# A table of places instead of a scheduler, from unit 8 on, and Pool's subtractions in halves

## The chip, the cores and the metric

The kernel runs on one core of a Trainium2 chip. The metric is the device time of one execution in microseconds; lower is better. A profile adds the busy time of each engine: TensorE (PE, with its weight loads as PEld), VectorE (DVE), ScalarE (ACT), GpSimd (POOL), and SP, which here only issues transfers.

## What is computed

A delta rule attention over 4 batches, 8 heads, 768 tokens of 48 numbers, and behind it a feed-forward layer (384 to 2048 to 384) with a rational function between its two products:

```python
for t in range(S):
    kt, vt, bt = (k_n[:, :, t], v[:, :, t], beta[:, :, t, None])
    y[:, :, t] = np.einsum('bhd,bhde->bhe', q[:, :, t], state)
    v_old = np.einsum('bhde,bhd->bhe', state, kt)
    state = state + bt[:, :, :, None] * np.einsum('bhd,bhe->bhde', kt, vt - v_old)
...
h = x @ w_in
h2 = h * h
h3 = h2 * h
P = a[0] + a[1] * h + a[2] * h2 + a[3] * h3
Q = 1.0 + np.abs(b[0]) * np.abs(h) + np.abs(b[1]) * h2
g = P / (Q + 1e-06)
return (g @ w_out).astype(np.float32)
```

`k_n` is `k` divided by its norm, and `x` is the attention's output with the heads side by side, 3072 rows of 384.

## The kernel before

**Tiling.** The 768 tokens are cut into 12 chunks of 64. One chunk of all four batches makes 256 rows for the feed-forward layer, whose 2048 hidden columns are cut into 8 units of 256. So there are 96 units, numbered through; unit 27 is unit 3 of chunk 3. Every number is kept as a pair of float16 (a rounded part and what is left), and a product of two such pairs is three matmul passes (`PASSES`).

**A unit.** `hidden` (L806) makes the first product in 18 matmuls into `ph`. `numerator` gives ScalarE two instructions (L826, L827) and a third (L829), and VectorE three (L828, L830, L831); `quotient` gives ScalarE Ln and Exp (L839, L840), VectorE L842 (which writes the first half of `mg`), L843 and L844, and Pool L845 (the second half of `mg`). `accumulate` (L860) is the second product, 12 matmuls in three groups of four into `po`. L843 uses the `ph` of the next unit as scratch, so the first product of a unit two later waits until L844 has read it (two `ph` buffers). `in_order` keeps these VectorE instructions in the order in which they are written.

**Attention.** Each chunk runs ahead of the units that use it, in stages of some instructions on each engine. Keys: load `kw`, normalize (`keys_normalized`, L481 to L492), transpose (`ptk`, L448, with a correction by `minus16`, L464), move to block-diagonal form by a transfer (`kbd`), multiply (`pg`, L396), write to memory and read back in another layout (`gd`, `gb`). The inverse of 16x16 blocks on VectorE (L543 to L576) goes out and back through `img` and `wc`. Queries likewise (`ptq`, `pm`, `mm`). Then the recurrence: split the state (`sh`), residual (`pk`, `v`, `rr`), three solve steps and a last one (`pu`, `z`, L238), the new state (`pd`, L703), the outputs (`py`, `y`), and the tokens (L734 to L746), which find a scale for `x` in seven hand-overs between ScalarE, TensorE and VectorE. All attention products go through `mm3` (48 matmuls each, L396). `split16` (L228 to L241) makes the float16 pair: ScalarE rounds, and VectorE, or Pool where `eng=nc.gpsimd` is given, subtracts (L236).

**What sets the order.** The kernel is traced in loops: for each unit `n` the numerator of `n`, the quotient of `n - 1`, one step of the attention stages (`back`, `middle`, `front`, `ahead`, each for another chunk), the second product of `n - 2`, the first product of `n + 1`. The tracing framework then schedules all of it: it runs a list scheduler with its own estimate of each instruction's duration over the whole program and picks, engine by engine, what is ready, with `tc.high_priority` for the recurrence. So the order that the chip gets is that scheduler's, and it differs from chunk to chunk. Each engine works through its queue in order; transfers are issued by SP, in order too.

Of the kernel before, what the change touches and what calls it, by code (L numbers as in the profile page):

```python
# [36 lines left out]
def kernel(  # L37
# [191 lines left out]
    def split16(dst, src, scale=None, eng=None):  # L229
# [5 lines left out]
        if scale is None:  # L235
            (eng or nc.vector).tensor_sub(dst[1], src, dst[0])  # L236
        else:
            nc.vector.scalar_tensor_tensor(  # L238
                out=dst[1], in0=src, scalar=scale, in1=dst[0], op0=ALU.mult, op1=ALU.subtract
            )  # L240

# [800 lines left out]
```

## Time and profile before

| | us |
|---|---|
| median of 3 runs (lowest to highest) | 833.21 (831.11 to 839.61) |
| the profiled execution | 836.04 |
| its span, first to last instruction | 834.3 |
| busy: DVE, ACT, PE, POOL | 720.0, 652.7, 649.7, 296.4 |
| first ScalarE instruction of unit 0, 8, 80 | 148.5, 222.9, 749.6 |

Busy time is time with at least one instruction on the engine. Instructions of one engine overlap at their ends, so that a queue without gaps has its starts closer together than one instruction takes. The clock that TensorE was granted averaged 0.958 of full speed. The chain that ended last is followed back from the last instruction, at each step to what released it.

### The profile page before, as it was taken

The page shows a single profiled execution, that of the slowest core. Times are in us where ns is not written, and L with a number is a line of the kernel's source. Part 1 is how long each engine was busy: PE and PEld are TensorE (multiplying, and loading weights), DVE is VectorE, ACT ScalarE, POOL GpSimd, SP SyncE. Part 2 cuts the span into 40 slices and gives each one's busy share as a digit, 9 for nine tenths or more (in the row PEclk, how much of TensorE's full clock was granted, in tenths as well). Part 3 has the DMA queues.
Part 4 walks back from the last instruction along what each step waited for, and adds up shares of the span by engine and source line. Part 5 has one row for each costly group of instructions (what it writes and reads, how often), then busy time and mean ns, then how long its engine had stood idle before and what let it go on. Part 6 is the DMA issues. An engine that isn't in the chain of part 4 may idle for free.

```text
span 834.3 us, 23340 instructions
## 1 busy us (share of the span) xinstructions
PE 649.7 (78%) x9520; PEld 514.5 (62%) x9520; DVE 720.0 (86%) x1290; ACT 652.7 (78%) x1301; POOL 296.4 (36%) x263
## 2 busy tenths in 40 slices
PE   1323465677889788888988998889989988998995
PEld 1213454565677676666776776667858867686662
DVE  5787768988979888779998889999989898998996
ACT  4755678889877986878987978879879776887973
POOL 7451425225233443323513514522433231322232
PEclk9999975999989999999999999999999999999998
DMA  8977867566467646685467275275455353200000
GB/s 224 214 141 177 212 147 141 97 96 116 77 108 131 93 97 103 97 137 97 73 136 116 49 135 103 58 137 90 100 98 95 78 86 66 54 2 21 1 20 20
DMA packets 358411, 84.35 MB, mean 101 GB/s; under 512 B 349856, under 2 KB 352928, under 8 KB 358304
## 3 DMA queue, kind: packets, MB, share of 16 engines
q1 hardware_dynamic: 356128, 81.69, 52.0%
q8 instruction: 75, 1.23, 0.6%
q10 hardware_dynamic: 2176, 1.17, 0.5%
q14 instruction: 32, 0.26, 0.1%
HBM read 34.70 MB, written 13.65 MB: 58 GB/s over the span
## 4 chain that ended last, share of the span: by engine, by line
DVE 28%; PE 24%; DMA 18%; ACT 15%; SPq 7%; issue 5%; POOL 1%; POOLq 0%; ACTq 0%; DVEq 0%
PE ph L806 8%; PE po L860 6%; DVE ph L843 3%; PE pu L396 3%; DVE mx L831 3%; DVE mg L842 2%; DMA qw<-in_q_dram 2%; SPq L604 2%; SPq L122 2%; DVE mx L828 2%; DMA gd<-g 2%; DVE mx L844 2%; DVE mx L830 2%; DMA wc<-img 2%; DMA img<-wh 2%
## 5 line engine op out<-in xcount | busy, mean ns | idle before, releaser
L806 PE MATMUL ph<-xT,w_in 128*128 128x256 f16 x1728 | 214.4, 278 | 28.3 <-DVE mx L844 18.3
L860 PE MATMUL po<-w_out,mg 128*128 128x384 f16 x1152 | 222.7, 334 | 16.3 <-DVE mg L842 10.0
L845 POOL TENSOR_TENSOR mg<-mx 128x512 f16<-128x512 f32 x96 | 125.1, 1303 | 306.0 <-DVE mx L844 236.1
L806 PEld LDWEIGHTS <-w_in 128*128 128x128 f16 x1728 | 168.7, 100 | 62.2 <-issue 19.9
L860 PEld LDWEIGHTS <-mg 128*128 128x128 f16 x1152 | 108.2, 99 | 83.0 <-DVE mg L842 15.6
L828 DVE SCALAR_TENSOR_TENSOR mx<-mx,msc,ph 128x512 f32<-128x512 f32 x96 | 71.2, 742 | 23.9 <-ACT mx L827 18.8
L843 DVE SCALAR_TENSOR_TENSOR ph<-mx,msc,mg 128x512 f32<-128x512 f32 x96 | 84.3, 878 | 0.8
L396 PEld LDWEIGHTS <-kbd 128*128 128x128 f16 x1680 | 59.3, 102 | 38.4 <-issue 29.6
L829 ACT ACTIVATE mx<-mx 128x512 f32<-128x512 f32 x96 | 60.7, 632 | 27.8 <-DVE mx L828 27.5
L826 ACT ACTIVATE mx<-ph,msc 128x512 f32<-128x512 f32 x96 | 65.3, 680 | 13.7 <-PE ph L806 6.7
L842 DVE SCALAR_TENSOR_TENSOR mg<-mx,msc 128x512 f16<-128x512 f32 x96 | 74.9, 781 | 0.4 <-ACT mx L840 0.4
L827 ACT ACTIVATE mx<-ph,coef,msc 128x512 f32<-128x512 f32 x96 | 74.3, 774 | 0.0
L844 DVE SCALAR_TENSOR_TENSOR mx<-mx,msc,ph 128x512 f32<-128x512 f32 x96 | 71.3, 743 | 1.3
L831 DVE SCALAR_TENSOR_TENSOR mx<-mx,msc,ph 128x512 f32<-128x512 f32 x96 | 71.2, 741 | 1.0
L839 ACT ACTIVATE mx<-mx,msc 128x512 f32<-128x512 f32 x96 | 69.4, 723 | 1.4
L830 DVE TENSOR_TENSOR mx<-ph,mx 128x512 f32<-128x512 f32 x96 | 65.6, 684 | 0.0
L840 ACT ACTIVATE mx<-mx 128x512 f32<-128x512 f32 x96 | 60.5, 630 | 1.0
L396 PEld LDWEIGHTS <-ebd 128*128 128x128 f16 x1728 | 52.5, 99 | 10.6 <-issue 8.1
L396 PE MATMUL pu<-z,ebd 128*128 128x48 f16 x1728 | 53.5, 188 | 6.3 <-DMA ebd<-et 2.8
L396 PEld LDWEIGHTS <-wbd 128*128 128x128 f16 x1152 | 36.3, 100 | 19.5 <-issue 15.9
L236 POOL TENSOR_TENSOR mm<-m,mm 128x1024 f16<-128x1024 f32 x12 | 29.7, 2474 | 52.2 <-ACT mm L232 22.8
L396 PE MATMUL pg<-tk,kbd 128*128 128x64 f16 x576 | 24.2, 204 | 21.9 <-ACT nrm L486 7.8
(197 smaller groups left out, 1234.0 us busy)
## 6 DMA issues: line engine op xcount, KB each, us to landing
wsi<-in_moe_w_in_dram SPq DMA_DIRECT2D x8, 768.0 KB, 7.9
gd<-g SPq DMA_DIRECT2D x24, 256.0 KB, 3.5
wso<-in_moe_w_out_dram SPq DMA_DIRECT2D x8, 768.0 KB, 5.8
mbd<-mm SPq DMA_DIRECT2D x24, 256.0 KB, 4.9
wc<-img SPq DMA_DIRECT2D x24, 256.0 KB, 4.8
wbd<-wc SPq DMA_DIRECT2D x24, 256.0 KB, 4.8
knbd<-kn SPq DMA_DIRECT2D x44, 128.0 KB, 2.9
kw<-in_k_dram SPq DMA_DIRECT2D x48, 96.0 KB, 3.3
```

The costliest lines, as they stand in the source:

```text
L396: nc.tensor.matmul(dst[p][:, h], head(bd, lp, p * H + h), head(rt, rp, p * H + h), start=start and n == 0 and h == 0, stop=stop and n == l ...
L806: nc.tensor.matmul(ph[:, i], w_in[:, f2, wp, cc, i * P : (i + 1) * P], x[:, xp, cc], start=k == 0, stop=k == 3 * NCC - 1,)
L827: nc.scalar.activation(u, ph, AF.Identity, scale=A3, bias=a2)
L828: in_order(nc.vector.scalar_tensor_tensor(out=w, in0=z, scalar=B0, in1=ph, op0=ALU.add, op1=ALU.mult))
L830: in_order(nc.vector.tensor_mul(u, ph, u))
L831: in_order(nc.vector.scalar_tensor_tensor(out=u, in0=u, scalar=A1, in1=ph, op0=ALU.add, op1=ALU.mult))
L839: nc.scalar.activation(r, w, AF.Ln, bias=Q0)
L842: in_order(nc.vector.scalar_tensor_tensor(out=g[:, 0], in0=u, scalar=A0, in1=r, op0=ALU.add, op1=ALU.mult))
L843: in_order(nc.vector.scalar_tensor_tensor(out=t, in0=w, scalar=Q0, in1=g[:, 0], op0=ALU.add, op1=ALU.mult))
L844: in_order(nc.vector.scalar_tensor_tensor(out=u, in0=u, scalar=A0, in1=t, op0=ALU.add, op1=ALU.subtract))
L845: nc.gpsimd.tensor_mul(g[:, 1], u, r)
L860: nc.tensor.matmul(po[p], g[:, gp, i, p * P : (p + 1) * P], w_out[:, f2, wp, i], start=f2 == lo and i == 0 and k == 0, stop=f2 == hi - 1 a ...
```

## The change

Every stage becomes a generator that yields between its pieces, and a table gives each piece a place in units, relative to the chunk (`PLAN`) or to the unit (`UNIT`). All pieces of all chunks are sorted by place and traced in that order. Up to place 8 the framework's scheduler still orders them; from there on a `manual_schedule` for TensorE, VectorE, ScalarE and Pool keeps the traced order as it is. SP's transfers are still placed by the scheduler. The priorities are gone (`FIRST` is empty). The arithmetic stays the same; where Pool subtracts, it does so in two halves. Two small moves: in `numerator`, VectorE's multiplications that follow are now a stage of their own (`cubic`) and L830's counterpart comes ahead of L828's; and in the chunk's scales `v` is squared ahead of `q`.

```diff
         if scale is None:
-            (eng or nc.vector).tensor_sub(dst[1], src, dst[0])
+            n = src.shape[1] // 2
+            for sl in [slice(0, 2 * n)] if eng is None else [slice(0, n), slice(n, 2 * n)]:
+                (eng or nc.vector).tensor_sub(dst[1][:, sl], src[:, sl], dst[0][:, sl])
...
+    def halved(dst, src, scale=None, eng=None):
+
+        if scale is None:
+            nc.scalar.copy(dst[0], src)
+            yield
+            n = src.shape[1] // 2
+            for sl in [slice(0, 2 * n)] if eng is None else [slice(0, n), slice(n, 2 * n)]:
+                if eng is not None and sl.start:
+                    yield
+                (eng or nc.vector).tensor_sub(dst[1][:, sl], src[:, sl], dst[0][:, sl])
...
+    PLAN = {
+        "load_k": (-32.4564,),
...
+        "kbd": (-25.2603,),
...
+        "gram": (-24.5307, -24.311, -23.3642),
...
+        "tokens": (-4.308, -4.1793, -4.0913, -4.0867, -3.9637, -3.8515, -3.7149, -3.7003, -3.4793, -3.3379),
...
+    UNIT = {
+        "hidden": (-0.3166,),
+        "numerator": (0.0001, 0.3411, 0.9473),
+        "cubic": (0.3156, 0.5071),
+        "quotient": (1.343, 1.5094, 1.6629, 1.9614, 2.1316, 2.297),
+        "accumulate": (2.1777, 2.825, 3.0308, 3.1137),
+    }
...
+    def do(event):
+        t, nm, n, last, made = event
+        if not made:
+            made.append(STAGES[nm](n) or iter(()))
+        with tc.high_priority(FIRST[nm]) if nm in FIRST else nullcontext():
+            if last:
+                run(made[0])
+            else:
+                next(made[0], None)
+
+    events = [e for c in range(NCH) for e in of_chunk(c)] + [e for n in range(N) for e in of_unit(n)]
+    events.sort(key=lambda e: e[0])
...
+    upto = 8.0
+    for e in events:
+        if 0 <= e[0] < upto:
+            if e[1:3] == ("hidden", GRP):
+                tables(GRP, NU)
+                scalars(0, GRP, NU)
+            do(e)
+    if upto < N:
+        with tc.manual_schedule(engines={mybir.EngineType.DVE, mybir.EngineType.Activation, mybir.EngineType.PE, mybir.EngineType.Pool}):
+            for e in events:
+                if e[0] >= upto:
+                    do(e)
```

What this moves, at three places. In the names `z_5_1` is step 1 of chunk 5's solve, `mx29` and `mg29` belong to unit 29, and a last number counts buffers.

VectorE from unit 29's second instruction up to unit 30's first, before:

```order
L830 TENSOR_TENSOR mx29_6111<-ph_29_6092,mx29_6111 128x512
L238 SCALAR_TENSOR_TENSOR z_5_0_6300<-pu_5_6198,zmask_91,z_5_0_6300 128x768
L257 TENSOR_SCALAR sf_4_6060<-lgx4_6067 128x1
L756 RECIPROCAL kp_4_0_6125<-lgx4_6067 128x1
L831 SCALAR_TENSOR_TENSOR mx29_6111<-mx29_6111,msc_3_5028,ph_29_6092 128x512
L842 SCALAR_TENSOR_TENSOR mg28_6120<-mx28_6044,msc_3_5028 128x512
L739 RECIPROCAL sf_4_6060<-sf_4_6060 128x1
L482 TENSOR_REDUCE nrm_8_6770<-sq_8_6771 128x16
L843 SCALAR_TENSOR_TENSOR ph_29_6092<-mx28_6044,msc_3_5028,mg28_6120 128x512
L238 SCALAR_TENSOR_TENSOR xT_4_6058<-px_4_6062,sf_4_6060,xT_4_6058 128x768
L844 SCALAR_TENSOR_TENSOR mx28_6044<-mx28_6044,msc_3_5028,ph_29_6092 128x512
```

The same stretch now, from behind the third instruction of unit 29 to the first of unit 30:

```order
L858 RECIPROCAL kp_4_0_6062<-kp_4_0_6062 128x2
L257 SCALAR_TENSOR_TENSOR z_5_1_6248<-pu_5_6087,zmask_91,z_5_1_6248 128x768
L949 SCALAR_TENSOR_TENSOR mg28_6258<-mx28_6023,msc_3_5445 128x512
L616 TENSOR_TENSOR pr_6_5794<-ab_6_5795,wt0_121 128x64 x2
L621 TENSOR_REDUCE wt0_121<-pr_6_5794 128x2x4x4
L951 SCALAR_TENSOR_TENSOR ph_29_6068<-mx28_6023,msc_3_5445,mg28_6258 128x512
L610 TENSOR_TENSOR pr_6_5794<-gb_6_5738,wt0_121 128x512
L613 TENSOR_REDUCE ab_6_5795<-pr_6_5794 128x64
L953 SCALAR_TENSOR_TENSOR mx28_6023<-mx28_6023,msc_3_5445,ph_29_6068 128x512
L616 TENSOR_TENSOR pr_6_5794<-ab_6_5795,wt0_121 128x512
L621 TENSOR_REDUCE wt0_121<-pr_6_5794 128x8x8
L257 SCALAR_TENSOR_TENSOR z_5_2_6347<-pu_5_6087,zmask_91,z_5_2_6347 128x768
```

Two solve steps and most of chunk 6's inverse (`pr_6`, `ab_6`, `wt0`) now share one unit, and the same rows come back every 8 units.

ScalarE from unit 27's first instruction on, before:

```order
L826 ACTIVATE mx27_5932<-ph_27_5913,msc_3_5028 128x512
L827 ACTIVATE mx27_5932<-ph_27_5913,coef_105,msc_3_5028 128x512
L232 CAST mm_6_5648<-m32_6_5646 128x8x2x64
L461 CAST tk_7_5668<-ptk_7_5669 128x4x2x64 x2
L716 ACTIVATE y_4_5886<-py_4_5789,sc_4_3157 128x768
L829 ACTIVATE mx27_5932<-mx27_5932 128x512
L246 ACTIVATE xT_4_6058,xs_4_6059<-y_4_5886 128x768
L839 ACTIVATE mx27_5932<-mx27_5932,msc_3_5028 128x512
L826 ACTIVATE mx28_6044<-ph_28_6025,msc_3_5028 128x512
```

and now:

```order
L922 ACTIVATE mx27_5847<-ph_27_5755,msc_3_5445 128x512
L923 ACTIVATE mx27_5847<-ph_27_5755,coef_105,msc_3_5445 128x512
L488 CAST tq_6_5783<-ptq_6_5784 128x4x2x64 x2
L793 ACTIVATE y_4_5857<-py_4_5554,sc_4_3076 128x768
L497 CAST tq_6_5783<-ptq_6_5784 128x4x2x64 x2
L943 ACTIVATE mx26_5667<-mx26_5667,msc_3_5445 128x512
L945 ACTIVATE mx26_5667<-mx26_5667 128x512
L247 CAST kn1_117<-kw_78 128x4x2x48
L247 CAST rr_5_5979<-v_5_3899 128x768
L269 ACTIVATE xT_4_6000,xs_4_6001<-y_4_5857 128x768
L928 ACTIVATE mx27_5847<-mx27_5847 128x512
L922 ACTIVATE mx28_6023<-ph_28_5981,msc_3_5445 128x512
```

The queries' transposes, the outputs `y`, the residual's rounding and the squares of the tokens stand in one unit; the unit's own third instruction (L928) comes last, ahead of the next unit, and Ln and Exp of the unit before stand in the middle.

Pool around the same units, before:

```order
L845 TENSOR_TENSOR mg24_5465<-mx24_5320 128x512
L236 TENSOR_TENSOR mm_6_5648<-m32_6_5646,mm_6_5648 128x8x2x64
L845 TENSOR_TENSOR mg25_5731<-mx25_5456 128x512
L845 TENSOR_TENSOR mg26_5941<-mx26_5722 128x512
L236 TENSOR_TENSOR rr_5_5999<-v_5_3772,rr_5_5999 128x768
L845 TENSOR_TENSOR mg27_6053<-mx27_5932 128x512
```

and now:

```order
L253 TENSOR_TENSOR rr_5_5979<-v_5_3899,rr_5_5979 128x384
L955 TENSOR_TENSOR mg26_5977<-mx26_5667 128x512
L253 TENSOR_TENSOR rr_5_5979<-v_5_3899,rr_5_5979 128x384
L253 TENSOR_TENSOR kn1_117<-kw_78,kn1_117 128x2x2x48
L253 TENSOR_TENSOR mm_6_6152<-m32_6_6004,mm_6_6152 128x4x2x64
L955 TENSOR_TENSOR mg27_6066<-mx27_5847 128x512
L253 TENSOR_TENSOR mm_6_6152<-m32_6_6004,mm_6_6152 128x4x2x64
L955 TENSOR_TENSOR mg28_6258<-mx28_6023 128x512
```

The subtractions `mm` and `rr` are two instructions each, with a unit's own Pool instruction between the halves.

More of the change, by code (lines that the diff above doesn't have):

```diff
@@ L240, in split16, with run @@
             )
+    def halved(dst, src, scale=None, eng=None):
[8 more added lines that the diff above has]
+        else:
+            nc.scalar.activation(dst[0], src, AF.Copy, scale=scale)
+            yield
+            nc.vector.scalar_tensor_tensor(
+                out=dst[1], in0=src, scalar=scale, in1=dst[0], op0=ALU.mult, op1=ALU.subtract
+            )
+    def run(stage):
+        for _ in stage:
+            pass
     def parts(t):
@@ L582, in inverse @@
             )
+        yield
         im = img[c % NIMG]
@@ new lines @@
+    STAGES = {
+        "load_k": loading("k"),
+        "keys": keys_normalized,
+        "rows": keys_by_row,
+        "load_v": loading("v"),
+        "load_q": loading("q"),
+        "kbd": keys_transposed,
+        "gram": key_products,
+        "gl": key_product_halves,
+        "inverse": inverse,
+        "scales": scales,
+        "queries": queries_transposed,
+        "masked": query_products,
+        "gbd": gram_to_diagonal,
+        "blocks": off_blocks,
+        "wbd": inverse_to_diagonal,
+        "state": state_split,
+        "residual": residual,
+        "qbd": queries_to_diagonal,
+        "mbd": masked_to_diagonal,
+        "knbd": rows_to_diagonal,
+        "solve": solve,
+        "next": state_next,
+        "outputs": outputs,
+        "tokens": tokens,
+        "scalars": scalar_steps,
+        "numerator": numerator,
+        "cubic": cubic,
+        "quotient": quotient,
+        "accumulate": accumulate,
+        "hidden": hidden,
+    }
@@ new lines, in of_chunk, with of_unit @@
+    def of_chunk(c):
+        for nm, times in PLAN.items():
+            if c == 0 and nm in ("state", "qbd", "scalars") or c == NCH - 1 and nm in ("rows", "knbd", "next"):
+                continue
+            if c == 0 and nm == "residual":
+                times = times[2:]
+            made = []
+            for i, t in enumerate(times):
+                yield NU * c + t, nm, c, i == len(times) - 1, made
+    def of_unit(n):
+        for nm, times in UNIT.items():
+            made = []
+            for i, t in enumerate(times):
+                yield n + t, nm, n, i == len(times) - 1, made
@@ new lines @@
+    early = [e for e in events if e[0] < 0]
+    for nm in ("load_k", "load_q", "load_v"):
+        for e in early:
+            if e[1:3] == (nm, 0):
+                do(e)
+    early = [e for e in early if e[2] or e[1][:4] != "load"]
+    for e in early:
+        if e[2] == 0 and e[1] != "hidden":
+            do(e)
+    weights(0, GRP)
+    tables(0, GRP)
+    scalars(0, 0, GRP)
+    weights(GRP, NU)
+    for e in early:
+        if e[2] or e[1] == "hidden":
+            do(e)
+    upto = 8.0
```

350 lines of the change are left out of this document (180 added, 170 removed).

## The prediction

> **What bounds the kernel now.** I read the page's busy times first, then its chain, then the busy times in stretches cut at the first ScalarE instruction (L826) of units 8, 16, 24 and so on, one row for each chunk of eight units. The profiled execution took 836.04 us with a span of 834.3; the median of the runs is 833.21, so a sum made on the span is carried over as a difference.
>
> ```profile
> span 834.3 us, 23340 instructions
> PE 649.7 (78%) x9520; PEld 514.5 (62%) x9520; DVE 720.0 (86%) x1290; ACT 652.7 (78%) x1301; POOL 296.4 (36%) x263
> ...
> DVE 28%; PE 24%; DMA 18%; ACT 15%; SPq 7%; issue 5%; POOL 1%; POOLq 0%; ACTq 0%; DVEq 0%
> ```
>
> No engine bounds the whole: VectorE is busiest with 86%, but the chain that ends last passes through four engines, and a quarter of it (DMA 18%, SPq 7%) is transfers and the queue that issues them.
>
> ```profile
> core 0: us, PE busy (x) PEld busy (x) DVE busy (x) ACT busy (x) POOL busy (x), PEclk, DMA share, GB/s
> 222.90:288.50 65.60, 54.27 (x844) 43.17 (x841) 58.88 (x101) 52.58 (x104) 25.31 (x25) 0.95 0.69 115
> 288.50:356.30 67.80, 57.85 (x981) 47.30 (x982) 54.53 (x99) 54.57 (x106) 26.42 (x23) 1.00 0.56 96
> 356.30:416.50 60.20, 53.07 (x806) 41.50 (x803) 54.98 (x101) 50.16 (x102) 24.93 (x21) 0.97 0.61 101
> 416.50:475.40 58.90, 52.02 (x831) 42.09 (x829) 52.97 (x90) 49.48 (x97) 21.89 (x19) 0.97 0.58 101
> 475.40:537.10 61.70, 53.47 (x795) 42.74 (x790) 56.50 (x103) 49.22 (x101) 23.17 (x20) 0.94 0.51 97
> 537.10:593.30 56.20, 49.33 (x794) 40.17 (x790) 51.55 (x86) 47.32 (x95) 18.73 (x17) 1.00 0.59 106
> 593.30:647.50 54.20, 49.25 (x754) 39.34 (x752) 49.88 (x89) 46.23 (x91) 16.67 (x12) 0.97 0.53 100
> 647.50:706.10 58.60, 52.80 (x918) 42.87 (x915) 53.63 (x93) 44.61 (x84) 15.29 (x11) 0.97 0.43 78
> 706.10:749.60 43.50, 41.85 (x560) 32.88 (x559) 40.75 (x65) 36.52 (x69) 13.13 (x10) 1.00 0.14 32
> 749.60:787.30 37.70, 34.22 (x329) 24.46 (x327) 33.60 (x58) 32.19 (x64) 8.93 (x7) 1.00 0.05 12
> 787.30:834.30 47.00, 36.48 (x246) 23.16 (x244) 37.98 (x53) 28.03 (x44) 13.09 (x10) 0.94 0.07 17
> ```
>
> The reader is to see three things. Chunks 1 to 8 take 54.2 to 67.8 us each, 483.2 in all (60.4 each). TensorE, VectorE and ScalarE are all busy 45 to 58 us of that: three engines with nearly equal work. So the time of a chunk is decided by how well the order interleaves the three, which is what the change rewrites. From chunk 9 on little attention is left (chunk 10: 37.7 us with VectorE at 33.6), and there is little to win.
>
> **What the new order does to each unit.** Both kernels run the same arithmetic, so I price an order by what it puts between the starts of two neighbouring units on each engine. The price of an instruction is its spacing to the next one when that follows at once, since neighbours overlap:
>
> ```profile
> 575.57 0.74 DVE L842 SCALAR_TENSOR_TENSOR mg<-mx,msc 128x512 f16<-128x512 f32 x1
> 576.23 1.01 DVE L238 SCALAR_TENSOR_TENSOR xT<-px,sf,xT 128x768 f16<-128x768 f32 x1
> 577.16 0.75 DVE L843 SCALAR_TENSOR_TENSOR ph<-mx,msc,mg 128x512 f32<-128x512 f32 x1
> ...
> 571.09 0.67 ACT L826 ACTIVATE mx<-ph,msc 128x512 f32<-128x512 f32 x1
> 571.66 0.77 ACT L827 ACTIVATE mx<-ph,coef,msc 128x512 f32<-128x512 f32 x1
> 572.33 0.29 ACT L759 ACTIVATE kp<-top,kp 128x1 f32<-128x1 f32 x1
> ...
> 577.05 1.21 PE pu L396 x48
> 578.26 1.30 PE po L860 x8
> 579.56 1.01 PE pg L396 x34
> 580.57 1.97 PE ph L806 x18
> ```
>
> VectorE: 0.66 us for 128x512, 0.93 for 128x768. ScalarE: 0.57 and 0.67 for the first two of a unit. TensorE: 1.97 for a unit's first product (18 matmuls), 0.65 for four of the second, 1.21 for an attention product of 48. A unit alone is 6 x 0.65 = 3.9 on VectorE, 2.9 on ScalarE, 3.9 on TensorE.
>
> In the new order a chunk has the same eight places each time. By places 0 to 7, TensorE/VectorE/ScalarE in us: 5.1/4.9/3.2, 5.1/4.8/4.8, 5.1/6.0/4.9, 9.0/6.4/8.0, 4.8/7.0/5.1, 7.6/9.1/7.7, 5.1/4.9/7.1, 6.6/4.9/6.1. Two of them worked out: place 3 on TensorE, from unit 27's first product to unit 28's, holds 18 first-product matmuls (1.97), three groups of four second-product ones (1.95), eight transposes (0.87 at 0.109 each, as in the 18), three attention products of 48 (1.21 twice, and 1.4 for the wider one, as 34 of pg take 1.01) and four corrections with minus16 (0.44, at 0.109), 9.0 in all. Place 5 on VectorE is the second order piece of the change: with the three instructions of unit 29 ahead of it, six unit instructions (3.9), two 128x768 for the solve (1.86), and the eight instructions of the inverse (3.3), 9.1 in all. Taking the busiest engine of each place: 5.1 + 5.1 + 6.0 + 9.0 + 7.0 + 9.1 + 7.1 + 6.6 = 55.0 us a chunk.
>
> The old order, counted the same way, is ragged. Chunk 4, unit by unit, busiest engine: 6.9, 9.6, 5.6, 8.3, 5.6, 5.9, 6.0, 10.5, which is 58.4, against 58.9 measured (the row 416.50:475.40). Over chunks 1 to 10 it counts 545 (62.4, 62.7, 61.7, 58.4, 56.6, 56.4, 54.0, 53.6, 41.7, 37.8), and those chunks took 564.4, so waits add a factor of 1.035. The new order counts 515.4 there (55.5, then 54.9 five times, 54.4, 51.2, 44.5, 35.1); times 1.035 is 533.4, a gain of **31 us**. Units are not walls: queues let one engine's long unit overlap another's. If only pairs of units count, the old order is 519.9 and the new 504.5, the factor 1.086, the gain 16.7 us. If only whole chunks count, 473.3 and 463.0, factor 1.193, gain 12 us. The new gain lies between 12 and 31; I take **26**, nearer the single unit, whose factor is nearest to one and holds chunk by chunk.
>
> **The start.** Up to unit 8 the scheduler still orders the work, and the weight loads stand in the same order on the DMA queue. But the new order puts more in front of unit 8's first ScalarE instruction: 157.1 against 153.0 us on ScalarE, 154.1 against 151.9 on VectorE, 82.1 against 73.2 on TensorE, which has the room:
>
> ```profile
> 0.00:148.50 148.50, 57.29 (x823) 48.56 (x823) 108.60 (x219) 95.81 (x207) 65.27 (x73) 0.91 0.78 177
> 148.50:222.90 74.40, 57.80 (x887) 46.28 (x888) 66.19 (x141) 66.02 (x146) 23.60 (x21) 0.93 0.58 98
> ```
>
> TensorE is busy 115 of these 222.9 us, VectorE 175. The added work is what chunk 1 no longer holds. I take **+4 us** (0 to +9). The end (chunk 11: 36.4 against 37.1) I cost at nothing: the same units in the same order, VectorE and TensorE cover each other.
>
> **Pool's halves.** VectorE is held while Pool works, if it reads two operands from SBUF:
>
> ```profile
> 557.96 2.82 DVE L843 SCALAR_TENSOR_TENSOR ph<-mx,msc,mg 128x512 f32<-128x512 f32 x1
> 557.87 2.36 POOL L236 TENSOR_TENSOR mm<-m,mm 128x1024 f16<-128x1024 f32 x1 [1.21 <-ACT mm L232]
> L843 DVE SCALAR_TENSOR_TENSOR ph<-mx,msc,mg 128x512 f32<-128x512 f32 x96 | 84.3, 878 | 0.8
> L844 DVE SCALAR_TENSOR_TENSOR mx<-mx,msc,ph 128x512 f32<-128x512 f32 x96 | 71.3, 743 | 1.3
> L845 POOL TENSOR_TENSOR mg<-mx 128x512 f16<-128x512 f32 x96 | 125.1, 1303 | 306.0 <-DVE mx L844 236.1
> L236 POOL TENSOR_TENSOR mm<-m,mm 128x1024 f16<-128x1024 f32 x12 | 29.7, 2474 | 52.2 <-ACT mm L232 22.8
> ```
>
> L843 takes 2.82 us instead of 0.74 and ends 0.55 after Pool's instruction (560.23). L844, of the same shape but with one operand in PSUM, is never held, so L843's holds are 84.3 - 71.3 = 13 us. The Trainium skill, SBUF — State Buffer, section SBUF: two separate sides, calls the port pair that the two engines share an exclusive lock, held for the whole instruction while the loser fully blocks. By that rule, the trace agrees (L843 does its own 0.55 us after Pool's end). By the rule alone two halves back to back could hold L843 as long as one whole, and the term below would be 0 instead of -4 (the sum 811). A half costs Pool (2 x 1.303 - 2.474) = 0.13 us more, 58 times, 8 us; Pool is busy 15 to 26 us of a chunk, which hides it. The gain is at most half of the 13 us and some like it on smaller instructions, 10 us; at least 0, if Pool keeps the port. I take **-4**, since VectorE decides about half of the places.
>
> **New waits.** What is fixed now waits at the head of its queue. The transfers have room in the new order: kbd, issued at place 5.9 to 6.7 of a chunk, is needed at 7.5.
>
> ```profile
> kbd<-tk SPq DMA_DIRECT2D x24, 192.0 KB, 5.4
> ```
>
> At some 6.8 us a unit kbd has 1 us to spare behind its 5.4. I cost the transfers at nothing; without that cover TensorE stops at pg, with the next unit's first product behind it, at up to 5 us a chunk.
>
> **Sum:** -26 + 4 - 4 = -26, so a span of 808 and a median of 833.2 - 26 = **807 us**.
>
> **Rivals.** *The fixed queues stand still at the tokens' hand-overs (slower).* Squares, transpose, maximum, broadcast, logarithm and power go from ScalarE to TensorE to VectorE and back seven times; the new order has them all between places 3.69 and 4.29, 0.6 of a unit or 4 us, where the old one spreads them:
>
> ```profile
> 563.16 0.86 ACT L246 ACTIVATE xT<-y 128x768 f16<-128x768 f32 x1
> ...
> 571.94 0.15 DVE L739 RECIPROCAL sf<-sf 128x1 f32<-128x1 f32 x1
> ```
>
> That is 8.9 us with two other units in it. If three queues stand for the 4 us that the table allows, in 9 chunks, it costs 36: -26 + 36 = +10, 843. It decides from 26/9 = 2.9 us a chunk. Against it: the order leaves 128x512 instructions and matmuls of other units between most steps. *Nothing is won:* only the whole chunk counts (-12) and the start costs its upper bound (+9): 830. For it: both orders hold the same 48 us a chunk on the busiest engine. Against: chunk 7, among the most even of the old order (54.0), is the fastest of 1 to 8 (54.2). *The waits go too:* the factor 1.035 falls to 1.00, since DMA's and SPq's quarter of the chain has more room, and the cover of neighbouring units stays: 515.4 - 564.4 = -49, with +4 and -4, 784. That the change does not do what it says is ruled out by the order: all chunks from unit 8 on have the same rows.
>
> **How the numbers follow.** My forecast has 0.60, the waits gone 0.14, nothing won 0.13, standing queues 0.13. The range takes in the fast rival and goes most of the way to the slow one: 778 to 838, whose low end lies 6 below the fast rival; the forecast's own range is 790 to 822. A measurement of this kernel tells about 1% from no change (8 us): faster 0.74, same 0.13, slower 0.13.
>
> **What would show it.** Right: chunks 2 to 7 within 1 us of each other at 55 to 58 us; unit 8 at 223 to 232; L843's mean below 830 ns; DMA and SPq below a fifth of the chain. Wrong: chunks over 60 with ScalarE and TensorE idle in front of the tokens' instructions, TensorE waiting for kbd in each chunk, or unit 8 later than 235.

## The result, and the profile after

The kernel with the change takes **789.93 us** (median of 4 runs, 789.29 to 790.87), the kernel before 832.16 beside it (831.0 to 839.61, 4 runs): a ratio of 0.9476, with an interval of 0.9418 to 0.9533. The profiled execution took 790.87 us with a span of 789.1, so 45.2 us of span are gone. 807 was predicted, with 778 to 838 as the range.

The page after: busy times and the chain that ended last.

```profile
span 789.1 us, 23451 instructions
PE 639.4 (81%) x9520; PEld 510.7 (65%) x9520; DVE 712.7 (90%) x1290; ACT 661.9 (84%) x1301; POOL 313.9 (40%) x321
...
DVE 41%; PE 20%; ACT 6%; DMA 3%; issue 3%; SPq 0%; POOLq 0%; ACTq 0%; DVEq 0%
```

This chain could be followed back only to 204.45 us, so its shares add up to 73%. Within that, DMA and SPq are 3 of 73, a twenty-fifth, where they were a quarter.

The stretches, cut as before at the first ScalarE instruction (now L922) of a unit: the start, chunk 0, chunk 1, chunk 4, the end, and chunks 1 to 10 in one row. The two rows of the second block are the kernel before, up to unit 8 and chunks 1 to 10.

```profile
core 0: us, PE busy (x) PEld busy (x) DVE busy (x) ACT busy (x) POOL busy (x), PEclk, DMA share, GB/s
0.00:141.90 141.90, 58.74 (x821) 48.98 (x821) 109.80 (x219) 97.00 (x212) 71.70 (x86) 0.70 0.86 190
141.90:228.80 86.90, 63.17 (x1065) 52.93 (x1064) 69.82 (x143) 69.88 (x146) 26.77 (x29) 0.84 0.59 96
228.80:283.00 54.20, 51.21 (x810) 41.20 (x809) 52.86 (x97) 49.51 (x96) 23.52 (x24) 1.00 0.52 99
390.70:444.40 53.70, 50.34 (x805) 40.69 (x804) 52.36 (x95) 50.48 (x100) 23.50 (x24) 1.00 0.61 111
743.10:789.10 46.00, 35.90 (x251) 23.57 (x249) 37.24 (x53) 29.05 (x46) 13.08 (x10) 0.98 0.07 18
228.80:743.10 514.30, 481.60 (x7389) 385.17 (x7388) 495.87 (x877) 465.99 (x900) 202.40 (x197) 1.00 0.50 94
```

```profile
0.00:222.90 222.90, 115.09 (x1710) 94.85 (x1711) 174.79 (x359) 161.83 (x351) 88.87 (x94) 0.92 0.72 151
222.90:787.30 564.40, 498.13 (x7568) 396.52 (x7566) 507.26 (x880) 462.88 (x908) 194.47 (x160) 0.98 0.50 88
```

Chunks 1 to 10 go from 564.4 to 514.3 us, **-50.1**; unit 8 starts 5.9 us later; the end is 1.0 shorter; together -45.2. The -50.1 can be split on VectorE: its busy time fell by 11.4 us (507.26 to 495.87) and its unoccupied time by 38.7 (57.1 to 18.4). Some of the 11.4 is work that only moved: ahead of unit 8 VectorE is now busy 179.62 us against 174.79. It is now busy for 52.4 of a chunk's 53.7 us. Chunks 1 to 7 last 53.7 to 54.2 us, all alike.

What VectorE waited for from unit 8 on, longest totals first (us in total, times, longest), before and after:

```profile
DVE mx L828 <- ACT mx L827: 17.7, 17, 2.4
DVE sc L615 <- PE pfq L253: 8.4, 5, 4.6
```

```profile
DVE xs L814 <- PE px L812: 7.4, 10, 1.4
DVE z L257 <- ACT z L255: 1.3, 3, 0.7
```

The ragged waits of a unit's own instructions are gone. What is left is mainly one wait at one place: the tokens' reduction L814 waits 0.7 us in nearly every chunk for TensorE's transpose.

Three of the eight places of chunk 4: place 3, place 5, place 7.

```profile
405.60:414.70 9.10, 9.10 (x189) 8.08 (x187) 8.39 (x12) 8.60 (x16) 5.81 (x6) 1.00 0.72 126
420.30:429.40 9.10, 7.83 (x124) 6.38 (x120) 8.86 (x22) 8.11 (x17) 3.88 (x3) 1.00 0.58 109
437.30:444.40 7.10, 6.46 (x86) 4.79 (x84) 7.00 (x15) 6.64 (x14) 1.27 (x1) 1.00 0.32 47
```

In place 3 TensorE is busy without a gap, in places 5 and 7 VectorE nearly so. The two long places cost what the count gave them (9.0 and 9.1, measured 9.1 and 9.1). The other six are off by up to 1.4 us, either way (place 4: 7.0 counted, 5.6 measured; place 6: 7.1 counted, 7.9 measured).

The group that replaces L843:

```profile
L951 DVE SCALAR_TENSOR_TENSOR ph<-mx,msc,mg 128x512 f32<-128x512 f32 x96 | 73.8, 769 | 1.2
```

### The profile page after: what moved, and what is told of

Its sections match the earlier page's. It is cut to its first block, busy times and chain, and to the rows that moved or that the text cites. A ratio compares the mean times of both kernels' runs of the same rounds, so it can differ in the third digit from the quotient of the medians.

```text
span 789.1 us, 23451 instructions
## 1 busy us (share of the span) xinstructions
PE 639.4 (81%) x9520; PEld 510.7 (65%) x9520; DVE 712.7 (90%) x1290; ACT 661.9 (84%) x1301; POOL 313.9 (40%) x321
## 3 DMA queue, kind: packets, MB, share of 16 engines
q1 hardware_dynamic: 356128, 81.69, 53.7%
## 4 chain that ended last, share of the span: by engine, by line
DVE 41%; PE 20%; ACT 6%; DMA 3%; issue 3%; SPq 0%; POOLq 0%; ACTq 0%; DVEq 0%
PE ph L902 8%; DVE ph L951 5%; DVE mg L949 5%; DVE mx L953 4%; PE po L969 4%; DVE mx L936 4%; DVE mx L926 4%; DVE mx L934 4%; DVE z L257 3%; PE py L422 2%; ACT mx L923 2%; PE pm L422 1%; DMA gd<-g 1%; DVE pr L597 1%; DVE pr L616 1%
## 5 line engine op out<-in xcount | busy, mean ns | idle before, releaser
L955 POOL TENSOR_TENSOR mg<-mx 128x512 f16<-128x512 f32 x96 | 129.0, 1344 | 327.5 <-DVE mx L953 175.4
L969 PE MATMUL po<-w_out,mg 128*128 128x384 f16 x1152 | 218.0, 327 | 10.9 <-DVE mg L949 5.7
L902 PE MATMUL ph<-xT,w_in 128*128 128x256 f16 x1728 | 209.1, 276 | 12.2 <-DVE mx L953 8.6
L969 PEld LDWEIGHTS <-mg 128*128 128x128 f16 x1152 | 106.3, 98 | 72.1 <-DVE mg L949 10.9
L922 ACT ACTIVATE mx<-ph,msc 128x512 f32<-128x512 f32 x96 | 65.5, 683 | 21.2 <-PE ph L902 19.0
L949 DVE SCALAR_TENSOR_TENSOR mg<-mx,msc 128x512 f16<-128x512 f32 x96 | 75.4, 785 | 1.3 <-ACT mx L945 1.2
L951 DVE SCALAR_TENSOR_TENSOR ph<-mx,msc,mg 128x512 f32<-128x512 f32 x96 | 73.8, 769 | 1.2
L953 DVE SCALAR_TENSOR_TENSOR mx<-mx,msc,ph 128x512 f32<-128x512 f32 x96 | 71.2, 742 | 1.6
L934 DVE TENSOR_TENSOR mx<-ph,mx 128x512 f32<-128x512 f32 x96 | 65.5, 682 | 6.4 <-ACT mx L923 6.2
L926 DVE SCALAR_TENSOR_TENSOR mx<-mx,msc,ph 128x512 f32<-128x512 f32 x96 | 70.8, 738 | 0.0
L928 ACT ACTIVATE mx<-mx 128x512 f32<-128x512 f32 x96 | 60.1, 626 | 11.6 <-DVE mx L926 11.6
L253 POOL TENSOR_TENSOR mm<-m,mm 128x512 f16<-128x512 f32 x24 | 33.9, 1419 | 28.4 <-ACT mm L247 19.2
L255 ACT ACTIVATE z<-pu,zmask 128x768 f16<-128x768 f32 x36 | 32.7, 910 | 11.3 <-PE pu L422 10.6
L422 PEld LDWEIGHTS <-wbd 128*128 128x128 f16 x1152 | 34.3, 99 | 11.0 <-issue 6.7
```

What stands on the lines that cost most here:

```text
L422: nc.tensor.matmul(dst[p][:, h], head(bd, lp, p * H + h), head(rt, rp, p * H + h), start=start and n == 0 and h == 0, stop=stop and n == l ...
L902: nc.tensor.matmul(ph[:, i], w_in[:, f2, wp, cc, i * P : (i + 1) * P], x[:, xp, cc], start=k == 0, stop=k == 3 * NCC - 1,)
L926: in_order(nc.vector.scalar_tensor_tensor(out=w, in0=z, scalar=B0, in1=ph, op0=ALU.add, op1=ALU.mult))
L934: in_order(nc.vector.tensor_mul(u, ph, u))
L949: in_order(nc.vector.scalar_tensor_tensor(out=g[:, 0], in0=u, scalar=A0, in1=r, op0=ALU.add, op1=ALU.mult))
L951: in_order(nc.vector.scalar_tensor_tensor(out=t, in0=w, scalar=Q0, in1=g[:, 0], op0=ALU.add, op1=ALU.mult))
```

## The experiments

**Theory A** was: the fixed order takes the waits away and carries nearly all of the gain; Pool's halves are small. The rivals: the halves carry much of it; or the sequence in which the stages are written does it, without being fixed. Later runs ask what a chunk of 53.7 us is bound by. (The expectations call the scheduler the planner.) All runs in one table; the time before beside them was 833.7 in e1 to e4, 834.91 in e5 to e8, 834.58 in e9 to e11 and 833.85 in e12. The last two columns are from one profiled execution of each, which can lie some us beside the median (e5's, at 784.03, is the lowest of its four; e1's, at 802.8, the highest).

| run | median us | ratio to before (interval) | unit 8 at | chunks 1 to 10 |
|---|---|---|---|---|
| before | 832.16 | 1 | 222.9 | 564.4 |
| the change | 789.93 | 0.9476 (0.9418 to 0.9533) | 228.8 | 514.3 |
| e1 whole subtractions | 800.97 | 0.9593 (0.9535 to 0.9651) | 228.2 | 526.8 |
| e2 before, halves alone | 837.86 | 1.0039 (1.0003 to 1.0074) | 231.4 | 558.9 |
| e3 sequence not fixed | 835.36 | 1.0012 (0.9974 to 1.0051) | 231.8 | 557.6 |
| e4 fixed from unit 48 | 817.25 | 0.9799 (0.9737 to 0.9861) | 231.6 | 538.5 |
| e5 one hold out | 787.33 | 0.9421 (0.9392 to 0.945) | 226.1 | 510.2 |
| e6 three holds out | 781.91 | 0.9365 (0.9336 to 0.9394) | 227.5 | 506.5 |
| e7 and the hand-over | 781.21 | 0.9351 (0.9316 to 0.9385) | 229.4 | 505.9 |
| e8 fixed from unit 4 | 789.76 | 0.946 (0.9427 to 0.9493) | 228.8 | 515.9 |
| e9 all holds out | 778.96 | 0.9334 (0.9297 to 0.9371) | 229.1 | 502.8 |
| e10 products left out, place 3 | 792.14 | 0.9499 (0.9461 to 0.9538) | 230.8 | 512.6 |
| e11 products left out, place 7 | 802.83 | 0.9632 (0.9592 to 0.9671) | 241.4 | 514.0 |
| e12 the wait filled | 779.94 | 0.935 (0.9323 to 0.9377) | 229.4 | 502.6 |

### Is it the order or the halves?

**e3: the new text, nothing fixed.**

```diff
-    upto = 8.0
+    upto = 200.0
```

> The changed kernel's text throughout, its stages written out in the table's sequence and with halves, but no place from unit 8 on is fixed: the planner orders every engine again, as it does in the first eight units. Theory A (fixing the order is what takes the waits away): chunks unequal again, 55 to 68 us, DMA and SP's queue back at a tenth or more of the chain, 815 to 840 us. Rival B (to write the stages in this sequence and in small pieces is enough, the planner keeps to it): 788 to 798 us with chunks 1 to 7 near 54.

835.36 us. Busy times, chain, and chunks 1 to 10 of it:

```profile
PE 653.0 (78%) x9520; PEld 521.2 (62%) x9520; DVE 708.5 (85%) x1290; ACT 654.1 (78%) x1301; POOL 316.2 (38%) x321
...
DVE 27%; ACT 19%; DMA 18%; PE 17%; issue 8%; SPq 6%; POOL 4%; POOLq 0%; ACTq 0%; DVEq 0%
```

```profile
231.80:789.40 557.60, 494.34 (x7340) 395.41 (x7339) 487.96 (x868) 456.14 (x890) 196.37 (x186) 0.98 0.48 85
```

Theory A holds: DMA and SPq are back at 24% of the chain, VectorE is without work for 69.6 us of chunks 1 to 10 (18.4 in the change), and the chunks differ again (57.1 to 62.6 for chunks 1 to 8). VectorE's busy time there, 487.96, is no longer than the change's 495.87, so what fixing the order takes away is time in which VectorE stands without work. Writing the stages in the table's sequence, in small pieces, with halves, gains nothing measurable; fixing them does.

**e1: the change with whole subtractions.**

```diff
-            n = src.shape[1] // 2
-            for sl in [slice(0, 2 * n)] if eng is None else [slice(0, n), slice(n, 2 * n)]:
-                if eng is not None and sl.start:
-                    yield
-                (eng or nc.vector).tensor_sub(dst[1][:, sl], src[:, sl], dst[0][:, sl])
+            (eng or nc.vector).tensor_sub(dst[1], src, dst[0])
+            if eng is not None:
+                yield
```

> The changed kernel with one piece of the change undone: each of Pool's subtractions is one instruction again, at the place in the order where its first half stands. Theory A (the gain is the fixed order's, the halves are small): the halves were put at -4 us (0 to -10), so this gives 794 us (790 to 800), and VectorE's operations that meet one of Pool's long subtractions (mm, qw, gl) end up to 0.8 us later than now, 58 times in all. Rival B (a good part of the 42 us is the halves'): 803 us or more, with VectorE's longest hold back at 2 us and more.

800.97 us: 11 us back, between the two. Its chunk 4, its chunks 1 to 10, and the place where it loses most (L593 is the change's L597, L247 its L253):

```profile
394.90:450.10 55.20, 50.49 (x805) 40.67 (x804) 53.88 (x95) 50.68 (x99) 22.94 (x19) 1.00 0.60 108
...
228.20:755.00 526.80, 485.76 (x7393) 387.67 (x7392) 506.21 (x876) 467.47 (x901) 197.42 (x160) 0.99 0.50 92
```

```profile
480.44 2.21 DVE L593 TENSOR_TENSOR pr<-wt,ab 128x4 f32<-128x4 f32 x1
479.76 2.86 POOL L247 TENSOR_TENSOR mm<-m,mm 128x1024 f16<-128x1024 f32 x1 [1.88 <-ACT mm L245]
```

A product of 128x4 takes 2.21 us, since it ends when Pool's whole subtraction `mm` ends (482.62). With the half it took 1.12. VectorE's busy time in chunks 1 to 10 is 506.21, about that of the kernel before (507.26); it falls by 10.3 to 495.87 with the halves. Nearly all of that is this one product, here in e1's chunks 1 to 10 and in the change's:

```profile
L593 DVE TENSOR_TENSOR pr<-wt,ab 128x4 f32<-128x4 f32 (+2 forms) x24 | 20.5, 853 | 0.8
...
L597 DVE TENSOR_TENSOR pr<-wt,ab 128x4 f32<-128x4 f32 (+2 forms) x24 | 11.0, 459 | 0.8
```

So of the -50.1, the order with whole subtractions gives 564.4 - 526.8 = **37.6** and the halves 526.8 - 514.3 = **12.5**. The split goes by this path and is not one of independent parts: fixing the order of e3, which has the halves already, takes 557.6 - 514.3 = 43.3 us out of the chunks and 45.4 out of the median. The order does its part without shorter holds: by the sum of what VectorE's instructions take beyond the tenth percentile of their own shape, where that is over 0.1 us, VectorE was held 32.6 us behind Pool after unit 8 before the change, 31.9 in e1 and 20.7 in the change. (0.9 us of the 12.5 may be the clock: e1's chunk 5, granted 0.97, took 56.1 us, and its neighbour 55.2.)

**e2: the kernel before with the halves alone.**

```diff
-            (eng or nc.vector).tensor_sub(dst[1], src, dst[0])
+            n = src.shape[1] // 2
+            for sl in [slice(0, 2 * n)] if eng is None else [slice(0, n), slice(n, 2 * n)]:
+                (eng or nc.vector).tensor_sub(dst[1][:, sl], src[:, sl], dst[0][:, sl])
```

> The kernel before with one piece of the change alone: Pool's subtractions in halves, one behind the other, everything else as before. Theory A: 832 less 4 us, 828 (822 to 832): VectorE was held 32.6 us behind Pool after unit 8 and half of the holds behind subtractions can go. Rival B (the halves carry a good part of the gain): 818 or less. Rival C (a hold lasts as long as both halves, since Pool goes on without a gap): 832 to 836, nothing won, and Pool's 0.13 us more for each half seen.

837.86 us, 1.0039 (1.0003 to 1.0074): nothing won, as rival C says, though above its 832 to 836. But rival C's reason is not shown: VectorE's total hold behind Pool after unit 8 fell from 32.6 to 27.4 us (the same sum). Chunks 1 to 10 were 5.5 us shorter (558.9) while unit 8 came 8.5 us later; but VectorE was busy 4.6 us more ahead of unit 8 (179.4 against 174.8) and TensorE 5.7, so that much of the 5.5 may be work that only moved to the start. Whether the halves are worth anything in the scheduler's order stays open.

Nor does a hold last over both halves as a rule. In e3, where two halves of `mm` stand without a gap (first row both, second row the second half alone):

```profile
323.09 2.96 POOL L253 TENSOR_TENSOR mm<-m,mm 128x512 f16<-128x512 f32 x2
...
324.32 1.73 POOL L253 TENSOR_TENSOR mm<-m,mm 128x512 f16<-128x512 f32 x1
```

```profile
323.19 1.73 DVE L951 SCALAR_TENSOR_TENSOR ph<-mx,msc,mg 128x512 f32<-128x512 f32 x1
```

L951 ends at 324.92, 0.55 us after the first half's end (324.37), and Pool's second half takes 1.73 instead of the 1.28 that an undisturbed one takes: each waits for the other's running instruction, and VectorE gets in between. Over all fourteen traces, from 100 us on, an instruction of VectorE on `mg`, `ph`, `wh`, `pr` or `ab` that was running when the first of two adjoining Pool instructions ended got through ahead of the second's end in 147 of 156 places. The nine others began within 0.1 us of the first one's end, as in e2, where one that began 0.05 us before it waited for the second half too and took 1.82 us.

**e4: fixed from chunk 6 on.**

```diff
-    upto = 8.0
+    upto = 48.0
```

> The changed kernel with the table's order fixed from unit 48 (chunk 6) on instead of unit 8; in chunks 1 to 5 the planner orders the stages as they are written. Theory A (each chunk gains by itself as against the planner's order, and the planner's chunks 1 to 5 take 314 us as before, where the fixed ones take 269): 830 us (822 to 838), chunk 7 on at 53.7 as now. Rival B (the gain is the same 5 us in each chunk, 1 to 10 alike): 815 us. Rival C (the planner is as good once the stages are written in this sequence): 788 to 797.

817.25 us. Chunks 1 to 5 under the scheduler, then chunk 6 and chunk 7 fixed:

```profile
231.60:522.10 290.50, 255.58 (x3915) 206.06 (x3914) 257.44 (x465) 242.29 (x473) 110.01 (x109) 0.98 0.55 98
522.10:578.70 56.60, 51.16 (x842) 41.57 (x839) 50.88 (x92) 52.13 (x100) 22.20 (x23) 1.00 0.61 106
578.70:632.40 53.70, 50.34 (x805) 40.69 (x804) 52.36 (x95) 49.66 (x97) 21.13 (x20) 1.00 0.55 104
```

Rival B's 815 is nearer than theory A's 830. The fixed order is in its rhythm after one chunk (56.6, then 53.7), and the gain comes in every chunk: 21.2 us over chunks 1 to 5 (290.5 against the change's 269.3). I had taken the scheduler's chunks 1 to 5 from the kernel before, 314; on the new text it makes 290.5 of them.

**e8: fixed four units earlier.**

```diff
-    upto = 8.0
+    upto = 4.0
```

> The changed kernel with the order fixed from unit 4 on instead of unit 8. Units 4 to 7 take 23 us under the planner (behind a unit 3 of 32 us in which the experts' weights are still being made) and 29.7 us in the table's rhythm (places 4 to 7 of a chunk). Theory A (the start is bound by the weights' work, which the fixed order cannot shift into gaps): unit 8 later by 0 to 10 us, 795 us (790 to 800). Rival B (chunk 0 loses 12.5 us because the planner runs ahead there, and fixing it earlier gives that back): 783 or less.

789.76 us, unit 8 at 228.8 as in the change: no difference. Unit 3 now takes 20.9 us and units 4 to 7 take 31.5, where it was 32.0 and 22.8. Rival B falls; theory A's 795 overstated the loss.

### What bounds a chunk now?

The chain in chunk 4 after the change runs on TensorE from place 3's first product to its end and then on VectorE to the end of place 7. (The profile leads its chain through the transfers `img` and `gd` in places 7 and 0, but ScalarE has no gap for them there; it waits 0.35 us for TensorE's `ph`, ahead of which `pd` waited for VectorE's `z`.) In that stretch VectorE is held at two spots, and in place 2 at a third. The one in place 7:

```profile
439.89 1.49 DVE L627 SCALAR_TENSOR_TENSOR wh<-wt,wh 128x256 f16<-128x256 f32 x1
439.80 1.27 POOL L955 TENSOR_TENSOR mg<-mx 128x512 f16<-128x512 f32 x1 [4.15 <-ACT sf L849]
```

**e5** moves this operation behind two that read PSUM.

```diff
-        "inverse": (..., -17.7935, -16.8416, -16.3475, -14.0101),
+        "inverse": (..., -17.7935, -16.655, -16.3475, -14.0101),
```

> The changed kernel with one number of the table moved: the inverse's last two VectorE operations (wh, L626 and L627) stand behind the next unit's first two (L934, L926, which read PSUM) instead of ahead of them, so that L627 no longer starts just when Pool begins the product mg, behind which it was held 1.04 us in every chunk. Theory A (from unit 8 on VectorE is the bound, back to back through 52.4 of a chunk's 53.7 us, so that a hold is paid in full): 1.0 us a chunk less for the 8 chunks that show it, 782 us (780 to 785). Rival B (the chunk's length comes from TensorE's full place 3 and from waits, VectorE's holds are covered): 789 to 791.

```profile
436.88 0.45 DVE L627 SCALAR_TENSOR_TENSOR wh<-wt,wh 128x256 f16<-128x256 f32 x1
```

```profile
386.80:440.00 53.20, 50.31 (x810) 40.76 (x806) 51.53 (x95) 50.43 (x100) 23.53 (x24) 1.00 0.63 112
```

The hold of 1.04 us is gone (1.49 to 0.45), the chunk is 0.5 shorter (53.7 to 53.2). So neither theory: of the hold 0.8 us shows, in place 0 (4.3 to 3.5), and places 1 and 2 give 0.3 of it back. These rows are from the execution of 784.03 us, with a start 2.7 us shorter than the change's; the three others took 787.2 to 787.8, and what they differ by was not profiled.

**e6** takes two more holds away: `pr` behind the first half of `mm` (0.96 us a chunk) and L949 behind the scaling `qw` (0.51).

```diff
-        "keys": (-30.4988, -30.4954, -30.416, ...),
+        "keys": (-30.4988, -30.4954, -29.975, ...),
-        "inverse": (..., -17.7935, -16.8416, -16.3475, -14.0101),
+        "inverse": (..., -17.7935, -16.655, -16.3475, -14.0101),
-        "masked": (-20.5558, -20.2308, -19.113, -18.8225, -17.827),
+        "masked": (-20.5558, -20.2308, -19.113, -18.7, -16.69),
```

> As e5, and two more holds taken away by the table's numbers: Pool's two halves of mm stand behind the products mg of places 5 and 7 (VectorE reads PSUM there) instead of beside the inverse's first small products (pr held 0.96 us a chunk), and Pool's scaling qw stands ahead of the keys' small nrm step (mg L949 held 0.51 us a chunk). Theory A (VectorE is the bound, holds are paid in full): 2.5 us a chunk, 8 chunks, less than now, 770 us (767 to 774), chunks near 51.2. Rival B (the longest engine of each place binds: without holds the sum over the eight places is 52.1): 1.6 us a chunk, 777 us. Rival C (the holds are covered, or a place moved makes a new wait of DMA or ScalarE): 787 or more.

781.91 us, chunks of 52.4: 1.3 us less, nearest to rival B's 1.6. The edit made a hold of its own: the second half of `mm` now runs just where `wh` had been moved to (L627 takes 1.38 us again). So 2.51 - 0.93 = 1.58 us of holds went and 1.3 came back as time. Pieces of its chain in one chunk, in order (start, us, what):

```profile
389.05 2.12 PE ph L902 x18
391.17 0.65 PE po L969 x4
...
408.57 1.97 PE ph L902 x18
410.53 0.12 PE px L812
410.68 0.28 DVE xs L814
410.96 0.67 DVE ph L951
...
439.06 0.87 DVE z L253
```

From 389.05 to 410.65 every longer piece is TensorE's, from 410.68 to the next chunk every longer piece is VectorE's: theory A2, two stretches with an engine each.

**e7** lets VectorE do L951 before the reduction that waits.

```diff
-        "tokens": (-4.308, -4.1793, -4.0913, -4.0867, -3.9637, ...),
+        "tokens": (-4.308, -4.1793, -4.038, -4.037, -3.9637, ...),
```

(on top of e6)

> As e6, and the tokens' largest value (the reduction L814) stands one operation later on VectorE, behind the unit's L951, so that VectorE no longer waits 0.71 us for TensorE's transpose px in every chunk. Theory A (VectorE bound): 0.7 us a chunk less than e6, 5 to 6 us in all. Rival (place 3 is TensorE's, full for 9.1 of 9.1 us, and what VectorE gains there is lost again behind TensorE): within 1 us of e6.

The rival holds: chunks of 52.4, as in e6. The wait went to the next step of the tokens, L818, with 6.7 us where L814 had 7.3 in e6:

```profile
DVE xs L818 <- PE px L816: 6.7, 11, 0.7
```

**e9** puts `wh` ahead of L953, the second half of `mm` into place 6 and one half of `kn` into place 7.

```diff
-        "rows": (..., -24.889, -24.8104),
+        "rows": (..., -24.889, -24.69),
-        "inverse": (..., -17.7935, -16.655, -16.3475, -14.0101),
+        "inverse": (..., -17.7935, -16.9, -16.3475, -14.0101),
-        "masked": (-20.5558, -20.2308, -19.113, -18.7, -16.69),
+        "masked": (-20.5558, -20.2308, -19.113, -18.7, -17.69),
```

(against e6)

> As e6, with the collision that e6 itself made taken out: the inverse's wh stands ahead of the unit's L953, so that it is done before Pool can begin mg; Pool's second half of mm stands in place 6 and one half of kn (0.57 us) in place 7, where VectorE reads PSUM. In e6 wh was held 0.93 us a chunk behind that half. Theory A2 (a chunk is two stretches, places 0 to 3 TensorE's, end to end for 21.6 us, and places 4 to 7 VectorE's; a hold counts in full in VectorE's stretch alone, and qw's hold in place 2 counted nothing): 0.9 us less a chunk than e6's 52.4, so 51.5, 7 us in all, 775 us (772 to 778). Rival (VectorE's time is given back to TensorE at the start of the next stretch, as half of e5's was): 0.4 a chunk, 778 to 780.

```profile
387.90:439.80 51.90, 50.07 (x809) 41.01 (x808) 50.06 (x95) 50.34 (x100) 23.09 (x24) 1.00 0.63 115
```

778.96 us, chunks of 51.8 where nothing disturbs (52.7 and 53.0 in chunks 3 and 6, in place 4, for a reason that stays open). No hold behind Pool is left from unit 8 on but one of 0.3 us. 0.6 of the 0.93 came back: in the chunks between the two, in the median the rival's. The intervals of e9 and of the change do not overlap, so this is a better table than the change's.

**e10 and e11** leave 16 matmuls out, once in TensorE's stretch and once in VectorE's. In e10 the small part of the queries is missing in `pm`, in e11 that of the keys in `pg`.

```diff
-        mm3(pm, d["kbd"], d["tq"])
+        mm3(pm, d["kbd"], d["tq"], passes=PASSES[:2])
```

```diff
-        mm3(pg, d["kbd"], d.pop("tk"))
+        mm3(pg, d["kbd"], d.pop("tk"), passes=PASSES[:2])
```

> The changed kernel with a third of one product left out: pm (queries by keys, in place 3 of each chunk) runs two of its three passes of 16 matmuls, so the small part of the queries is missing in it; 16 matmuls are 0.5 us of TensorE. Theory A2 (in places 0 to 3 TensorE sets the time): 0.5 us less in each chunk, place 3 at 8.6 instead of 9.1, chunks at 53.2, 785 us. Rival B (VectorE alone sets a chunk's length): chunks stay at 53.7, 789 to 791.

> The counterpart to e10: the same number of matmuls of the same shape left out of pg (keys by keys, in place 7 of each chunk), whose small part is missing then. Theory A2 (in places 4 to 7 VectorE sets the time): nothing, chunks stay at 53.7, 789 to 791. Rival C (TensorE's total sets a chunk's length): 0.5 us less in each chunk as in e10, 785 us.

Place 3 of a chunk in e10, place 7 in e11:

```profile
407.00:415.80 8.80, 8.73 (x172) 7.53 (x170) 8.35 (x12) 8.47 (x16) 5.79 (x6) 1.00 0.73 132
```

```profile
449.60:456.70 7.10, 6.16 (x70) 4.38 (x68) 7.00 (x15) 6.64 (x14) 1.27 (x1) 1.00 0.32 46
```

In place 7 the time does not move by a tenth (7.1, chunks of 53.7), so TensorE's total does not set a chunk's length. In place 3 it goes from 9.1 to 8.8 and the chunk from 53.7 to 53.5: theory A2's sign, with less than half of its 0.5 us. The 16 matmuls were priced too high: TensorE's busy time fell by 0.33 us a chunk (50.34 to 50.01). ScalarE is busy 8.47 of those 8.8 us and VectorE 8.35, so they are close behind. The medians say nothing of this: they are 2 and 13 us above the change's, because unit 8 starts at 230.8 and 241.4, though the edits take only 64 and 80 of some 1880 matmuls from the start.

**e12** fills VectorE's wait with the inverse's seven small operations, on top of e9.

```diff
-        "inverse": (-21.7996, -21.1241, -19.1862, -18.9795, ...),
+        "inverse": (-21.7996, -21.1241, -20.15, -18.9795, ...),
```

> As e9, and the inverse's first seven small VectorE operations (L593 to L598, 1.4 us) stand in place 3 ahead of the tokens' reduction L814, where VectorE waits 0.7 us for TensorE in every chunk, instead of in place 5; gb, which they read, had landed 10 us before. Theory A2 (VectorE's stretch, places 4 to 7, is shortened by 1.4 us and the hand-over is later by 0.7): 0.7 us less a chunk than e9's 51.8, so 51.1, and unit 8 to the end 5 us shorter. Rival D (after e9 the three engines are all full: in a chunk TensorE is busy 50.1, VectorE 50.1, ScalarE 50.3 of 51.9 us, and in place 5 ScalarE 8.17 of 8.20, so ScalarE takes over at once): 51.7 to 51.9, no gain, or a later hand-over makes it 52 and more.

Rival D holds: chunks of 52.2 where nothing disturbs, 502.6 us for chunks 1 to 10 against e9's 502.8, 779.94 us. What VectorE waited for, e9 and e12:

```profile
DVE xs L814 <- PE px L812: 7.3, 10, 1.4
...
DVE z L257 <- ACT z L255: 4.5, 9, 1.0
```

```profile
DVE z L257 <- ACT z L255: 10.1, 19, 1.3
```

L814's wait is out of the list's first rows, and the solve steps wait for ScalarE's rounding instead. After e9 TensorE, VectorE and ScalarE are each busy 50.1 to 50.3 of 51.9 us, and in e7 and e12 a shift between them only moved the wait.

## Why the prediction was right in sign and short in size

- **What bounds the kernel: right.** The interleaving was what a chunk's time hung on: with the new text and halves but no fixed order (e3) nothing is gained.
- **The order of units, -26: the term that was mis-sized.** With whole subtractions it measured -37.6, and the count with single units at the old factor gave -31 as the most. The step that failed is the factor: 1.035 was carried over from the scheduler's chunks as if waits were a share of any order. Nor does it hold chunk by chunk, as the prediction says: by its own counts it goes from 0.98 (chunk 3) to 1.09 (chunks 5 and 8), so the waits stood in some chunks and not in others. A table that repeats has its hand-overs with room in every chunk, and the waits went: 526.8 against the counted 515.4 is 1.022 with Pool's whole subtractions in it, and 514.3 is 0.998 with halves. That pairs and whole chunks pulled the value down from 31 to 26 was a step in the wrong direction. That the count without a factor meets the sum so closely is in part luck: chunks 1 to 7 took 376.8 us where it has 384.4, chunks 8 to 10 took 137.5 where it has 130.8, and e9, with the same pieces at nearly the same places, took 502.8.
- **Pool's halves, -4: too small.** 11 us in the median (800.97 to 789.93), 12.5 in the chunks, just beyond the -10 that was the most. The prediction took less than half of those 10, since VectorE decides about half of the places. But the holds fell by 11.2 us (31.9 to 20.7) and were paid in full: 9.5 of it is that of `pr`, which stands in VectorE's stretch at the same spot of every chunk (place 5 of chunk 4 takes 10.3 us in e1 and 9.1 in the change). `wh`, which is held behind `mg`, gained nothing from the halves. The bound of 0 from the exclusive lock (the Trainium skill, SBUF — State Buffer, section SBUF: two separate sides) does not apply: the lock is held for one instruction, the trace agrees (ends 0.55 us after the half), but VectorE gets in between two halves even when they stand without a gap (e3, and 147 of the 156 places counted there).
- **The start, +4: right in sign, its cause not shown.** +5.9, within 0 to +9. More work does stand ahead of unit 8, as counted (VectorE busy 179.62 against 174.79 us there, TensorE 121.90 against 115.09). But the start under the scheduler moved between 226.1 and 241.4 us in kernels that differ by a few numbers of the table or 16 matmuls a chunk, so 5.9 is within that scatter. VectorE does not set it: e1's is busy 184.1 us there, 4.5 more than the change's, and its unit 8 comes at 228.2.
- **The end, 0:** -1.0.
- **New waits, 0: right, its margin not.** From place 6.7 to 7.5 is 0.8 x 6.8 = 5.4 us, which leaves kbd's 5.4 no room, and not 1 us; from 5.9 it leaves 5.5. TensorE waited for kbd 4 times, all ahead of unit 8; none of it recurs.

```profile
PE pg L422 <- DMA kbd<-tk: 14.4, 4, 4.4
```

- **The rivals.** The tokens' hand-overs do make a standing wait, as the slow rival said, but of 0.7 us a chunk and not 4; in e7 and e12, where it was moved or filled, nothing was won. *The waits go too* was the nearest, 784, and its -49 for chunks 1 to 10 is the measured -50.1; by e1 this is two things, 37.6 of order and 12.5 of halves, not waits alone.
- **What would show it.** Unit 8 at 228.8 (223 to 232 said), L951's mean 769 ns (below 830), DMA and SPq below a fifth: as said. Chunks 2 to 7 within 1 us of each other: within 0.3, at 53.7 to 53.9 where 55 to 58 was said.

TensorE's clock, granted at 0.98 before and 1.00 after in these chunks, is a rival for a part of the order's 37.6 us only. Chunks 2 and 6 had 1.00 in both kernels and the change took 14.1 and 2.3 us out of them, 8.2 on average; out of the six others of 1 to 8, granted 0.94 to 0.97 before, it took 6.2 on average. An estimate of the most that it can be worth: what those rows lack to 1.00, times TensorE's busy time, is about 12 us before and 1.5 after (chunk 8, 0.97). What stays open: how much of that was paid; what makes the start scatter.

## What to carry to other kernels

Price a fixed, repeating order by the longest engine of each place, with no factor for waits taken over from a scheduler's order, and give the sum a few per cent to either side: counted 515.4, it measured 526.8 with whole subtractions, 514.3 with halves and 502.8 with the holds moved away. In such an order a hold of VectorE behind Pool recurs at the same spot in each period, so put Pool's long instructions beside VectorE operations that read PSUM, and look into which engine's stretch a hold falls before counting it in full. Compare such variants by the rows of their steady stretches: their medians carried a start that moved by up to 15 us for small edits.
